# Attention weights of the first step and feed-forward weights of the last: transfers taken in turn, at most two or three large ones in flight

## The chip, the cores and the metric

One core of one Trainium2 chip. The metric is the device time of one execution in microseconds (us); lower is better. The granted clock, that is the share of TensorE's full clock that the throttle lets through, was 0.98 to 1.00 on the mean.

## The reference

Two passes over the same weights: attention with a recurrent memory, then a SwiGLU feed-forward. The attention goes through 64 segments of 32 tokens one after the other, 8 memory tokens in front of each, 32 heads of 128, model width 576, all weights bf16. Cut to what matters:

```python
def _A_ref(x, mem0, Wq, Wk, Wv, Wo, seg_len):          # 64 segments, in order
    for s in range(n_seg):
        h = jnp.concatenate([mem, xs], axis=1)         # 8 + 32 tokens, 576 wide
        q = jnp.einsum('btd,dhe->bhte', h, Wq)         # Wq, Wk, Wv: 576 x 32 x 128
        k = ...; v = ...
        ...                                            # masked softmax, o = p v
        o = jnp.einsum('bhte,hed->btd', o, Wo)         # Wo: 32 x 128 x 576
        mem = o[:, :M, :]
def _B_ref(x, w1, w3, w2):                             # 576 -> 4608 -> 576
    return jnp.einsum('bsf,fd->bsd', silu(x w1) * (x w3), w2)
x = x + _A_ref(_layernorm(x), ...)
x = x + _B_ref(_layernorm(x), ...)
x = x + _A_ref(_layernorm(x), ...)
x = x + _B_ref(_layernorm(x), ...)
```

## The kernel before

The kernel keeps all attention weights on the core and works in steps: one segment of each attention layer, the second layer seven steps behind the first, with feed-forward units between them to fill TensorE. The order of all instructions is planned ahead; small methods record them, so nearly every TensorE instruction has one source line (L538 before, L540 after the change) and every transfer of SyncE another. A transfer goes out in program order on SyncE's queue. There are two stretches that the change touches. At the **start**, SyncE issues all attention weights: 19 MB, without which the first step cannot go on. At the **end**, once Wv, Wq/Wk and Wo have been read for the last time, their places are loaded with the feed-forward weights of the last step, nine units of 1.77 MB:

```python
    def dma(self, out, in_):
        self.ch("SP", self.nc.sync.dma_start(out=out, in_=in_))
...
    def load_qk(self, kind):                       # Wq (0), then Wk (1)
        def f(n):
            wd = (self.a.wq, self.a.wk)[kind]
            for c in range(4):                     # four chunks of 128 rows, 1 MiB each
                self.dma(self.T.W[:, 4 * kind + c, :], wd[c * P:(c + 1) * P, :])
            self.dma(self.T.W[kind * R64:(kind + 1) * R64, 8, :], wd[4 * P:D, :])   # tail of 64 rows
        return f
...
    def load_o(self, g):                           # four of 1.18 MB
        return lambda n: self.dma(self.T.WO[:, g * GH:(g + 1) * GH, :],
                                  self.a.wo[g * GH:(g + 1) * GH].rearrange("h e d -> e h d"))
...
    def tail_load(self, i, what):                  # unit i of 9, last step
        def f(n):
            ...                                    # t13, t2: places in WV, W or WO
            if what != 1:
                for kind, wd in ((0, self.a.w1), (1, self.a.w3)):      # two of 512 KB
                    self.dma(t13[:, 4 * kind:4 * kind + 4], wd[0:4 * P, fa:fa + 512].rearrange("(c p) f -> p c f", p=P))
                for kind, wd in ((0, self.a.w1), (1, self.a.w3)):      # two small tails
                    self.dma(t13[kind * R64:(kind + 1) * R64, 8], wd[4 * P:D, fa:fa + 512])
            if what != 0:                                              # one of 576 KB
                self.dma(t2, self.a.w2[fa:fa + 512, :].rearrange("(b p) d -> p b d", p=P))
            ...
```

## Time and profile before

| | before |
|---|---|
| median of 3 runs | 2802.13 us (2796.95 to 2804.0) |
| profiled span | 2798.6 us |
| TensorE (PE) busy | 2730.5 us, 98% of the span |
| first matmul on the fourth Wk chunk | 26.86 us |
| first value matmul of step 1 (a mark behind the whole start) | 66.96 us |
| DMA share and rate, 4 to 30 us | 1.01, 377 GB/s |
| DMA share and rate, 2746 to 2786 us | 1.10, 337 GB/s |

The lines that bound the kernel are in the prediction.

The timeline of PE (start, us busy, what, count, in brackets the idle time before and what ended it) shows the last Wk chunk:

```profile
26.86 2.22 PE L538 MATMUL bank<-HT,W 128*128 128x40 bf16 x58 [2.50 <-DMA W<-in_A_Wk_dram]
```

### The profile page before, as it was taken

How to read it: one execution, taken by the hardware profiler on the slowest of the kernel's cores; microseconds unless marked ns; L12 is line 12 of the kernel's file. 1: busy time of each engine (PE TensorE's matmuls, PEld its weight loads, DVE VectorE, ACT ScalarE, POOL GpSimd, SP SyncE). 2: the span in 40 equal slices, each digit the busy share in tenths (PEclk: the TensorE clock that was granted, in tenths of full speed). 3: DMA queues.
4: the chain of work that ended last, by engine and by line, in shares of the span. 5: the costliest groups of instructions: out<-in, count | busy, mean ns of one | idle time of the engine just before them, and what ended most of it. 6: DMA issues, size and time to landing. Idle time of an engine off the chain costs nothing.

```text
span 2798.6 us, 136339 instructions
## 1 busy us (share of the span) xinstructions
PE 2730.5 (98%) x60909; PEld 2252.9 (81%) x60909; DVE 2018.1 (72%) x5501; ACT 1116.7 (40%) x3422; POOL 328.4 (12%) x399
## 2 busy tenths in 40 slices
PE   5999999999999999999999999999999999999998
PEld 4787878888888888888888888888888788888886
DVE  4677777777777677777767777776777777677765
ACT  2434443443434344343434434343443434343332
POOL 1111110110101011010101101010110101010110
PEclk9999999999999999999999999999999999999999
DMA  8072524234251523425152342515234251423568
GB/s 306 17 197 83 162 67 138 65 112 130 62 153 48 152 73 111 132 60 153 49 148 77 111 131 60 150 52 145 81 111 131 60 147 54 142 82 109 143 177 248
DMA packets 483438, 323.80 MB, mean 116 GB/s; under 512 B 26297, under 2 KB 478401, under 8 KB 481185
## 3 DMA queue, kind: packets, MB, share of 16 engines
q1 hardware_dynamic: 479824, 308.15, 37.6%
q8 instruction: 476, 7.80, 1.2%
q0 software_dynamic: 3024, 6.93, 0.8%
q14 instruction: 114, 0.93, 0.1%
HBM read 310.26 MB, written 2.36 MB: 112 GB/s over the span
## 4 chain that ended last, share of the span: by engine, by line
PE 96%; DMA 1%; ACT 1%; issue 1%; DVE 1%; POOL 0%; SPq 0%; DVEq 0%; ACTq 0%; POOLq 0%
PE bank L538 83%; PE YB L538 14%; DMA W<-in_A_Wk_dram 1%; ACT HT L541 0%; DMA W<-in_A_Wq_dram 0%; ACT OT L541 0%; DVE STAT L544 0%; DVE SME L544 0%; DVE PB L544 0%; ACT PTS L541 0%; DVE HTT L544 0%; ACT SME L541 0%; DVE PTS L544 0%; DVE XR L544 0%; DVE XN L544 0%
## 5 line engine op out<-in xcount | busy, mean ns | idle before, releaser
L538 PEld LDWEIGHTS <-W 128*128 128x128 bf16 (+1 forms) x29040 | 1227.2, 98 | 158.8 <-issue 53.6
L538 PE MATMUL bank<-HT,W 128*128 128x80 bf16 (+3 forms) x22720 | 815.5, 198 | 20.4 <-DMA W<-in_A_Wk_dram 11.7
L538 PE MATMUL bank<-XTB,W 128*128 128x256 bf16 (+3 forms) x6320 | 654.6, 262 | 1.4 <-issue 1.3
L895 POOL MEMSET PB<- 128x1024 bf16 x284 | 270.0, 951 | 2119.2 <-PE bank L538 1682.6
L541 ACT ACTIVATE QKT<-bank 128x64 bf16<-128x64 f32 (+1 forms) x1381 | 316.1, 315 | 364.2 <-PE bank L538 335.5
L538 PE MATMUL YB<-OT,WO 128*128 128x80 bf16 (+3 forms) x11360 | 429.4, 199 | 20.6 <-ACT HT L541 13.5
L538 PEld LDWEIGHTS <-WO 128*128 128x128 bf16 (+1 forms) x11400 | 389.0, 101 | 55.8 <-issue 39.3
L538 PE MATMUL bank<-WV,HT 128*32 128x512 bf16 (+1 forms) x6840 | 384.4, 382 | 0.0
L544 DVE CAST QKT<-bank 128x64 bf16<-128x64 f32 (+2 forms) x683 | 186.2, 316 | 238.7 <-PE bank L538 236.7
L541 ACT ACTIVATE HTT<-bank 128x512 bf16<-128x512 f32 (+1 forms) x324 | 177.8, 551 | 392.9 <-PE bank L538 391.5
L538 PE MATMUL bank<-W2C,HTT 128*128 128x288 bf16 x2232 | 320.7, 287 | 0.4 <-DMA W2C<-in_B_w_dram 0.4
L544 DVE TENSOR_REDUCE STAT<-SME 104x8 f32<-104x320 f32 (+1 forms) x568 | 271.8, 479 | 51.3 <-ACT SME L541 47.0
L544 DVE TENSOR_TENSOR PB<-SME,STAT 40x128 bf16<-40x128 f32 (+1 forms) x1004 | 283.5, 321 | 15.5
L538 PEld LDWEIGHTS <-HT 128*32 128x32 bf16 (+1 forms) x6840 | 149.4, 95 | 166.8 <-issue 42.8
L538 PEld LDWEIGHTS <-HTT 128*128 128x128 bf16 x2304 | 206.4, 98 | 59.2 <-issue 6.9
L544 DVE SCALAR_TENSOR_TENSOR XR<-bank,XR 128x288 f32<-128x288 f32 x576 | 239.6, 448 | 11.7 <-PE bank L538 7.2
L544 DVE SCALAR_TENSOR_TENSOR HTT<-HTT,bank 128x512 bf16<-128x512 bf16 (+1 forms) x324 | 201.9, 623 | 55.4 <-ACT HTT L541 53.4
L541 ACT ACTIVATE PTS<-bank 128x320 bf16<-128x320 f32 (+1 forms) x413 | 157.1, 414 | 177.6 <-PE bank L538 120.9
L544 DVE TENSOR_TENSOR HTT<-HTT,bank 128x512 bf16<-128x512 bf16 (+1 forms) x324 | 203.5, 628 | 22.3 <-PE bank L538 0.5
L541 ACT ACTIVATE OT<-bank 128x320 bf16<-128x320 f32 (+1 forms) x379 | 147.0, 412 | 171.1 <-PE bank L538 170.9
L541 ACT ACTIVATE SME<-SME 104x320 f32<-104x320 f32 (+1 forms) x284 | 133.5, 470 | 202.5 <-DVE SME L544 202.3
L544 DVE TENSOR_TENSOR SME<-bank,maskb 104x320 f32<-104x320 f32 (+1 forms) x284 | 133.9, 485 | 104.6 <-PE bank L538 102.8
(64 smaller groups left out, 1671.4 us busy)
## 6 DMA issues: line engine op xcount, KB each, us to landing
W<-in_B_w_dram SPq DMA_DIRECT2D x612, 256.0 KB, 3.8
W2C<-in_B_w_dram SPq DMA_DIRECT2D x306, 288.0 KB, 3.2
W<-in_B_w_dram SPq DMA_DIRECT2D x612, 32.0 KB, 3.4
W<-in_B_w_dram SPq DMA_DIRECT2D x10, 512.0 KB, 8.7
WO<-in_A_Wo_dram SPq DMA_DIRECT2D x4, 1152.0 KB, 18.3
XR<-in_A_x_dram POOLq DMA_DIRECT2D x16, 288.0 KB, 4.6
W<-in_A_Wq_dram SPq DMA_DIRECT2D x4, 1024.0 KB, 8.0
W<-in_A_Wk_dram SPq DMA_DIRECT2D x4, 1024.0 KB, 16.8
```

What stands on the lines that cost most here:

```text
L538: self.ch("PE", self.nc.tensor.matmul(out, lhsT=lhsT, rhs=rhs, start=start, stop=stop, skip_group_check=True, **k))
L541: self.ch("ACT", self.nc.scalar.activation(*a, **k))
L544: self.ch("DVE", getattr(self.nc.vector, fn_)(*a, **k))
L895: return lambda n: self.ch("POOL", self.nc.gpsimd.memset(self.T.PB[:, pb.i], 0.0))
```

## The change

The intent: let the large loads of both ends go out in turn. A large transfer waits until the one two before it (at the start) or three before it (at the end) has landed, so that SyncE's queue never holds more than two or three of them and other traffic, the instruction blocks above all, has less ahead of it. Below such a wait is called a gate: of two at the start, of three at the end. A transfer has landed, or is home, when all its bytes have arrived. No instruction of a compute engine is added or moved.

```diff
@@ in the constructor
         self.tail_w = {}
+        self.turn = []
+        self.turn_dep = mybir.DependencyInfo(mybir.DependencyClass.Sync, mybir.DependencyReason.DATA)
@@
     def dma(self, out, in_):
-        self.ch("SP", self.nc.sync.dma_start(out=out, in_=in_))
+        return self.ch("SP", self.nc.sync.dma_start(out=out, in_=in_))
+
+    def dma_in_turn(self, out, in_, depth):
+
+        inst = self.dma(out, in_)
+        if len(self.turn) >= depth:
+            self.tc.add_manual_dep(inst.ins, self.turn[-depth].ins.name, self.turn_dep, reason="transfers in turn")
+        self.turn.append(inst)
@@ load_qk (load_v and load_o likewise, each with depth 2)
-                self.dma(self.T.W[:, 4 * kind + c, :], wd[c * P:(c + 1) * P, :])
+                self.dma_in_turn(self.T.W[:, 4 * kind + c, :], wd[c * P:(c + 1) * P, :], 2)
@@ tail_load (likewise t2, the 576 KB)
-                    self.dma(t13[:, 4 * kind:4 * kind + 4], wd[0:4 * P, fa:fa + 512].rearrange("(c p) f -> p c f", p=P))
+                    self.dma_in_turn(t13[:, 4 * kind:4 * kind + 4], wd[0:4 * P, fa:fa + 512].rearrange("(c p) f -> p c f", p=P), 3)
```

The tails of 64 rows keep plain `dma` and are not counted.

More of the change, by code (lines that the diff above doesn't have):

```diff
@@ L604, in f @@
             for c in range(4):
-                self.dma(self.wv(False)[:, c, :], self.a.wv[c * P:(c + 1) * P, :])
+                self.dma_in_turn(self.wv(False)[:, c, :], self.a.wv[c * P:(c + 1) * P, :], 2)
             t = self.a.wv[4 * P:D, :].rearrange("p (k r n) -> p k r n", k=2, r=2)
@@ L611, in load_o @@
     def load_o(self, g):
-        return lambda n: self.dma(self.T.WO[:, g * GH:(g + 1) * GH, :],
-                                  self.a.wo[g * GH:(g + 1) * GH].rearrange("h e d -> e h d"))
+        return lambda n: self.dma_in_turn(self.T.WO[:, g * GH:(g + 1) * GH, :],
+                                          self.a.wo[g * GH:(g + 1) * GH].rearrange("h e d -> e h d"), 2)
     def load_xn(self, g, xn):
@@ L658, in f @@
             if what != 0:
-                self.dma(t2, self.a.w2[fa:fa + 512, :].rearrange("(b p) d -> p b d", p=P))
+                self.dma_in_turn(t2, self.a.w2[fa:fa + 512, :].rearrange("(b p) d -> p b d", p=P), 3)
             for h in range(2):
```

## The prediction

> **What bounds the kernel now.** I read the page first, then the waits of TensorE over the whole span and in its two ends, then the DMA issues of those ends, one by one, and last the timeline and the granted clock there. The page's busy line and the chain that ended last say that TensorE (PE) is the bound:
>
> ```profile
> PE 2730.5 (98%) x60909; PEld 2252.9 (81%) x60909; DVE 2018.1 (72%) x5501; ACT 1116.7 (40%) x3422; POOL 328.4 (12%) x399
> ...
> PE 96%; DMA 1%; ACT 1%; issue 1%; DVE 1%; POOL 0%; SPq 0%; DVEq 0%; ACTq 0%; POOLq 0%
> PE bank L538 83%; PE YB L538 14%; DMA W<-in_A_Wk_dram 1%; ACT HT L541 0%; DMA W<-in_A_Wq_dram 0%; ACT OT L541 0%; DVE STAT L544 0%; DVE SME L544 0%; DVE PB L544 0%; ACT PTS L541 0%; DVE HTT L544 0%; ACT SME L541 0%; DVE PTS L544 0%; DVE XR L544 0%; DVE XN L544 0%
> ```
>
> The reader should see that no DMA wait reaches 2% of the chain. The change touches only loads of the first 60 us and the last 60 us, some 4% of the span between them; the 2680 us in the middle keep their instructions, waits and buffers. So what there is to win or lose must be in PE's waits in those two stretches. PE's waits, first of the whole span (cut), then of 0 to 62 us, then of 2738 us to the end:
>
> ```profile
> PE bank L538 <- DMA W<-in_A_Wk_dram: 11.7, 5, 4.4
> PE bank L538 <- issue: 7.6, 8, 2.7
> PE YB L538 <- issue: 3.0, 2, 1.9
> ...
> PE bank L538 <- DMA W<-in_A_Wk_dram: 11.7, 5, 4.4
> PE bank L538 <- DVE XN L544: 10.2, 1, 10.2
> PE bank L538 <- issue: 5.4, 3, 2.7
> ...
> PE bank L538 <- DVE XN L544: 3.4, 1, 3.4
> PE YB L538 <- issue: 1.9, 1, 1.9
> PE bank L538 <- issue: 1.1, 1, 1.1
> ```
>
> Columns: total us, times, longest. Two things stand out. PE waits 11.7 us for the key weights at the start. And of its 7.6 + 3.0 = 10.6 us of "issue" gaps (nothing that the profile shows held it back) 5.4 + 1.9 + 1.1 = 8.4 us lie in the 120 us in which the DMA engines are full. I take these gaps to be late instruction blocks; the page's queue list has that traffic: 476 packets, 7.80 MB, that is 16.4 KB each. This is presumably what the change is after.
>
> How the start is loaded, from the DMA issues (size of each, median us from issue to landing; windows of half a microsecond, so mostly one transfer):
>
> ```profile
> XN<-in_A_x_dram SPq DMA_DIRECT2D x1, 144.0 KB, 2.1
> ...
> W<-in_A_Wq_dram SPq DMA_DIRECT2D x1, 1024.0 KB, 4.8
> ...
> W<-in_A_Wq_dram SPq DMA_DIRECT2D x1, 1024.0 KB, 11.6
> ...
> W<-in_A_Wk_dram SPq DMA_DIRECT2D x1, 1024.0 KB, 14.9
> ...
> W<-in_A_Wk_dram SPq DMA_DIRECT2D x1, 512.0 KB, 20.4
> ```
>
> The latency grows with the place in the queue, so the queue is served in order: Wq chunks issued at 1.62 to 3.1 us land at about 6.4, 9.0, 11.5 and 14.7, Wk chunks at 19.2, 21.7, 24.2 and 26.8 (PE's matmuls on them start at exactly such times), the 64-row tail at 29.4. The spacing of 2.5 us for 1.05 MB is 420 GB/s, and the DMA share of these stretches is 1.02: full. SyncE does not have an endless queue even now: it waits 10.3 us for landings of Wk and 9.5 us of Wq before it issues Wv and Wo, so about 8 transfers are out at a time.
>
> **What the Trainium skill says.** (1) "DMA: Bandwidth & Descriptors", section "Queues, rings and completion order": each engine goes round-robin between queue rows at packet granularity. Then an instruction block waits for a packet or so of the weights, not for the whole weights' queue, and a shorter queue would help it little so long as it is never empty. The trace does not contradict it: a load has 8 to 20 us of queue ahead of it at the start, the stalls are at most 2.7 us. (2) Same page, "Anatomy of one DMA": a transfer has a fixed part of about 2 us beside its bytes, and a semaphore wait is served by the issuing sequencer before dispatch. The trace agrees: 144 KB at 420 GB/s moves in 0.35 us and landed after 2.1 us, so 1.75 us are fixed. (3) "Runtime: NRT & Kernel Launch", "Instruction fetch mechanics": instructions stream in 16 KiB blocks through a DMA queue of their own; the 16.4 KB packets agree. (4) "TensorE: Matmul & The Clock Gate", Part 1: the clock halves after idleness. The trace agrees: the granted clock is 0.50 from 40 to 45 us and 0.53 from 2760 to 2765.
>
> **The change part by part.** It removes nothing and adds no instruction that runs on PE, DVE or ACT. It adds waits on SyncE alone.
>
> Start: 12 chunks of 1.05 MB (Wq, Wk, Wv) and 4 of 1.18 MB (Wo), each waits until the one two before it has landed; tails go ungated behind them. Costs: does the queue run dry? Chunk j is issued when j-2 has landed; then j-1 is still moving. A lone chunk needs about 4.8 us (the first Wq row above). In flow, two chunks take 2 x 2.5 = 5.0 us. So with a wake-up and issue of 0.1 to 0.4 us the loop is 4.9 to 5.2 us against 5.0: between 0 and 0.2 us lost for a pair. Before PE's Wk wait ends there are 8 chunks, and the two tails (2.5 us each) refill the margin where they fall; I count +1 us, range 0 to 3, on the path. Gain: 4.5 of the 5.4 us of gaps sit at 33.9 (1.8) and 39.8 (2.7), after Wk has landed. Even if they vanished, PE would run into the next loads: Wv's fourth chunk lands at about 42.2 (issued 19.2, 23.0 to land) and PE starts on Wv at 44.0; Wo's last lands at 57.0 (issued 44.3, 12.7 to land) and PE reads it at about 58. So at most 1 to 2 us of those 4.5 can be had while the stream keeps its rate; with the round-robin rule I expect half of it, -1 us.
>
> End: 9 units of 1.77 MB, in each three large transfers (512, 512, 576 KB) gated three back, two small ones free. About one unit is in flight at a time; when its first part lands, 512 + 576 KB and more are still to move, 3.4 us at 330 GB/s, against 1.75 us fixed. The queue never runs dry: cost 0. What it could win is the 1.9 + 1.1 us of gaps. But the end is tied to the stream as well:
>
> ```profile
> 2778.88 0.52 SPq L547 DMA_DIRECT2D WO<-in_B_w_dram  x1
> WO<-in_B_w_dram SPq DMA_DIRECT2D x1, 512.0 KB, 8.6
> ...
> 2789.46 2.68 PE L538 MATMUL bank<-XTB,WO 128*128 128x128 bf16 x40
> ```
>
> The last unit's first part lands at 2787.5, its second (issued 2779.4, 9.7 to land) at about 2789.2; PE reaches the unit at 2789.46 and needs the second part four matmuls later. Slack: 0.4 us. Removing 3 us of gaps at 2746 to 2754 would only make PE wait here. -0.3 us.
>
> Sum: +1 - 1 - 0.3 = -0.3 us on a mean of the three runs of (2802.13 + 2796.95 + 2804.0) / 3 = 2801.0. **Predicted: 2801 us.**
>
> **Rivals.** (a) *The instruction fetch is freed and the loads speed up*: if long queues delay the fetches, and if 16 engines kept in step bring each chunk home earlier (by 29.4 us 10.1 MB had moved by the slices' rates, where 9.6 MB were needed, so half a megabyte of later loads, 1.1 us, ran ahead), then up to 4.5 + 3.0 + 1.1 = 8.6 us go: 2792. For it: the gaps lie almost wholly under full queues. Against it: Wv, Wo and the last unit have 0.4 to 2 us of slack. (b) *The gate becomes a new wait*: if landing to first byte takes 1 us more than I think, a chunk loses about 0.5 us, and the 8 to 16 gated chunks of the start cost 4 to 8 us, since every load there follows the last closely: 2805 to 2809. For it: 4.8 against 5.0 us is hardly any margin. Against it: the tails in between, and three in flight while they pass. (c) *All of it is hidden*: 2801.
>
> **Range and chances.** The three runs of before span 7 us alone. (a) and (b) are of like size and opposite sign, so 2793 to 2809 should hold it 8 times in 10. A 2% change is 56 us. The two ends together are 120 us and PE is busy for more than half of it, and all DMA waits and gaps there sum to some 22 us, so no reading reaches 56: faster 0.01, within 2% 0.98, slower 0.01.
>
> **What would show it.** Right: landings from issue of about 5 us for the start's chunks (not 8 to 21), but PE's matmuls on the last Wk chunk and tail within 2 us of 26.9 and 29.4; the wait of PE for Wk near 12 us; SyncE's waits for DMA grown; issue gaps in the first 62 us still 3 us or more; PE at the last unit between 2788 and 2791 relative to this trace. Wrong towards (a): gaps under 2 us in both ends, and the DMA's rate there above 420 and 330 GB/s. Wrong towards (b): the DMA share under 0.9 between 5 and 30 us, and Wk's tail after 32 us.

## More of the kernel before

The page's list of DMA issues gives for each group of transfers the size of each and the median us from issue to landing:

```profile
WO<-in_A_Wo_dram SPq DMA_DIRECT2D x4, 1152.0 KB, 18.3
...
W<-in_A_Wq_dram SPq DMA_DIRECT2D x4, 1024.0 KB, 8.0
W<-in_A_Wk_dram SPq DMA_DIRECT2D x4, 1024.0 KB, 16.8
```

A megabyte that is 17 us on its way at 420 GB/s has waited in a queue: it is the length of the queue that these figures show.

## The result, and the profile after

| | before | after |
|---|---|---|
| median of 4 runs each, same rounds | 2801.5 us (2796.95 to 2804.0) | 2806.02 us (2805.15 to 2807.35) |
| ratio after / before | | 1.0018, 95% interval 1.0001 to 1.0036 |
| profiled span | 2798.6 us | 2805.6 us |
| PE: fourth Wk chunk | 26.86 us | 30.99 us |
| PE: first score matmul | 30.89 us | 34.90 us |
| PE: first value matmul of step 1 | 66.96 us | 70.40 us |
| DMA share, 4 to 30 us | 1.01 | 0.93 |
| DMA share, 2746 to 2786 us | 1.10 | 1.01 |

Here and below a ratio is the mean time of one kernel's runs over the mean of the other's in the same rounds, so not quite the ratio of the medians. The change is "the same" within 2%, but about 5 us slower. All outputs are right.

The chain that ended last, after:

```profile
PE 94%; DMA 4%; ACT 1%; DVE 1%; issue 0%; SPq 0%; POOL 0%; DVEq 0%; ACTq 0%
```

Before, PE had 96% and DMA 1%. The 3% more are some 80 us: the chain now follows the loads through both ends, where it followed PE. That tells which way the bound runs there; it is not the size of the loss. PE's waits between 0 and 70 us, after (us in total, times, longest):

```profile
PE bank L540 <- DMA W<-in_A_Wk_dram: 12.3, 4, 4.5
...
PE bank L540 <- DMA W<-in_A_Wq_dram: 4.7, 2, 3.4
PE bank L540 <- issue: 4.2, 2, 2.9
```

The wait for Wk has hardly grown (11.7 before), but the wait for Wq has, from 1.7 to 4.7 us: the loss begins at the very first chunks. The gaps "issue" are still there. SyncE's own waits in the same stretch, after:

```profile
SPq L549 <- DMA W<-in_A_Wq_dram: 13.7, 4, 4.3
SPq L549 <- DMA WV<-in_A_Wv_dram: 11.7, 4, 4.3
SPq L549 <- DMA W<-in_A_Wk_dram: 11.2, 4, 4.3
SPq L549 <- DMA WO<-in_A_Wo_dram: 9.5, 3, 5.3
```

So the gates do what they should: SyncE now waits some 46 us for landings in place of 20, and the page's transfers are 7 to 8 us on their way in place of 8 to 18:

```profile
WO<-in_A_Wo_dram SPq DMA_DIRECT2D x4, 1152.0 KB, 8.3
W<-in_A_Wq_dram SPq DMA_DIRECT2D x4, 1024.0 KB, 7.3
W<-in_A_Wk_dram SPq DMA_DIRECT2D x4, 1024.0 KB, 7.1
```

7.1 and 7.3 us can be read as 2 x 2.5 us for two chunks in flight and 2.1 to 2.3 us of fixed time (an estimate from the spacing of 2.5 us). What that buys is in the timeline of PE, after, to set beside the line of before at 26.86:

```profile
17.79 0.21 PE L540 MATMUL bank<-HT,W 128*128 128x40 bf16 x1 [3.44 <-DMA W<-in_A_Wq_dram]
...
30.99 3.98 PE L540 MATMUL bank<-HT,W 128*128 128x40 bf16 x105 [3.31 <-DMA W<-in_A_Wk_dram]
```

The last Wk chunk comes 4.1 us later. The engines were not full all the time, as two of the stretches of 1 us show (length, busy us and count of PE, PEld, DVE, ACT, POOL, then granted clock, DMA share, GB/s). Before:

```profile
22.00:23.00 1.00, 0.00 (x0) 0.00 (x0) 0.00 (x0) 0.00 (x0) 0.00 (x0) 1.00 0.98 410
```

After:

```profile
22.00:23.00 1.00, 0.22 (x1) 0.11 (x1) 0.00 (x0) 0.00 (x0) 0.00 (x0) 1.00 0.08 33
23.00:24.00 1.00, 0.00 (x0) 0.00 (x0) 0.00 (x0) 0.00 (x0) 0.00 (x0) 1.00 0.49 123
```

A share of 0.08 is hardly more than one engine of 16 (0.06). The trace's records of single packets say the same: from 22.4 to 23.3 us only one packet at a time is in progress, 8 KB packets of 309 ns one after the other: one engine alone still moves its part of a chunk, and 15 engines have nothing, for the next chunk may not be issued before that last part is home. Packets take 309 ns in both kernels; no engine has become slower.

At the end, the last unit of the last step. The timeline of PE after (its counterpart before, 40 matmuls in one piece from 2789.46, is in the prediction):

```profile
2793.36 0.60 PE L540 MATMUL bank<-XTB,WO 128*128 128x128 bf16 x4 [2.31 <-DMA WO<-in_B_w_dram]
...
2794.84 3.93 PE L540 MATMUL bank<-XTB,WO 128*128 128x128 bf16 x36 [0.88 <-DMA WO<-in_B_w_dram]
```

and a stretch of the same execution:

```profile
2795.00:2800.00 5.00, 5.00 (x42) 3.75 (x41) 1.52 (x4) 0.77 (x2) 0.00 (x0) 0.50 0.02 7
```

PE waits 3.2 us for the weights of the last unit where it waited for none, and runs at a granted clock of 0.50 afterwards: 36 matmuls take 3.93 us where 40 took 2.68 before, and the next 8 on W 1.80 us in place of 1.15.

The 7.0 us between the two profiled executions, step by step: +3.4 at the start; -1.3 in the middle, where the execution of before has one gap of 1.1 us that the other lacks (chance: the instructions there are the same); -0.8 because PE's gaps at 2747 and 2754 are 1.4 + 0.8 us in place of 1.1 + 1.9; +0.3 up to the last unit; +3.2 of waiting there; +2.2 of halved clock. These sum to 7.0.

### The profile page after: what moved, and what is told of

Its sections match the earlier page's. It is cut to its first block, busy times and chain, and to the rows that moved or that the text cites. A ratio compares the mean times of both kernels' runs of the same rounds, so it can differ in the third digit from the quotient of the medians.

```text
span 2805.6 us, 136351 instructions
## 1 busy us (share of the span) xinstructions
PE 2733.6 (97%) x60909; PEld 2254.8 (80%) x60909; DVE 2018.9 (72%) x5501; ACT 1117.4 (40%) x3422; POOL 328.8 (12%) x399
## 4 chain that ended last, share of the span: by engine, by line
PE 94%; DMA 4%; ACT 1%; DVE 1%; issue 0%; SPq 0%; POOL 0%; DVEq 0%; ACTq 0%
PE bank L540 81%; PE YB L540 13%; DMA W<-in_B_w_dram 1%; DMA WO<-in_A_Wo_dram 1%; DMA W<-in_A_Wq_dram 1%; DMA WV<-in_A_Wv_dram 1%; DMA W<-in_A_Wk_dram 0%; ACT HT L543 0%; DMA WO<-in_B_w_dram 0%; ACT OT L543 0%; DMA WV<-in_B_w_dram 0%; DVE STAT L546 0%; DVE PB L546 0%; DVE SME L546 0%; DVE XR L546 0%
## 5 line engine op out<-in xcount | busy, mean ns | idle before, releaser
L540 PE MATMUL bank<-HT,W 128*128 128x80 bf16 (+3 forms) x22720 | 815.2, 198 | 22.3 <-DMA W<-in_A_Wk_dram 12.3
```

The costliest lines, as they stand in the source:

```text
L540: self.ch("PE", self.nc.tensor.matmul(out, lhsT=lhsT, rhs=rhs, start=start, stop=stop, skip_group_check=True, **k))
```

## The experiments

**The theory** after reading the two traces: a gate waits for the whole chunk, and a chunk is home when the slowest of its 16 engines is. "DMA: Bandwidth & Descriptors" of the Trainium skill, section "Why a DMA increments its semaphore by 16 and not by 1", says that each engine's last descriptor adds 1 to the semaphore after its own data; the trace agrees, with 16 packets of four bytes at the end of each transfer. As long as the queue is long, an engine that lags costs the others nothing, since they go on with the next chunk. With a gate of two there is a margin of only about 0.1 us (estimate: when a chunk lands the next has 2.5 us left to move, and the loop from landing over issue to the first bytes takes 4.9 - 2.5 = 2.4 us, by the lone chunks of g2 below), and every lag beyond it is idleness of all the other engines. It foretells that a gate one deeper, with a margin of 2.6 us, costs nothing.

**Rivals.** One: it is the start of the transfers that takes longer than reckoned (the loop, not the lag); then depth 1 must be slower than its own 4.8 us for each chunk. Two: only one of the two ends does harm. Three, on the gain that did not come: the gaps of PE have nothing to do with the DMA queues, or they have, and the gate of two or three leaves the engines just as full.

To weigh them I worked out, from each trace's records of single packets, how long an engine was idle on the mean of the 16, once in the start's stretch and once in the end's. (The records do not name the engine: idle is how far the number of packets in progress lies below 16. Counted more finely, the figures move by up to 0.1 us.)

| kernel (depth at start / end; - is no gate) | idle us, 4 to 56 us | idle us, 2746 to 2786 us | PE: fourth Wk chunk, us |
|---|---|---|---|
| before (- / -) | 0.00 | 0.00 | 26.86 |
| e3_deeper (4 / 6) | 0.00 | 0.01 | 27.64 |
| g4_one_more (3 / 4) | 0.02 | 0.24 | 28.65 |
| e2_tail_only (- / 3) | 0.01 | 2.51 | 29.82 |
| h2_tail_again (- / 3) | 0.00 | 2.33 | 27.30 |
| after (2 / 3) | 2.56 | 1.59 | 30.99 |
| g1_after_again (2 / 3) | 2.34 | 2.05 | 32.70 |
| e1_start_only (2 / -) | 4.17 | 0.08 | 31.30 |
| h1_start_again (2 / -) | 3.07 | 0.25 | 30.60 |
| g2_one_at_a_time (1 / 1) | 15.24 | (window holds other loads) | 40.88 |

And the times. "Difference" is the mean of the kernel's runs less the mean of the runs of before:

| kernel | median us (runs) | before, same rounds | difference us | ratio, 95% |
|---|---|---|---|---|
| e1_start_only | 2803.83 (5) | 2800.79 | +3.1 | 1.0011, 0.9999 to 1.0024 |
| h1_start_again | 2804.39 (5) | 2802.62 | +2.3 | 1.0009, 0.9995 to 1.0022 |
| e2_tail_only | 2800.87 (5) | 2800.79 | +1.4 | 1.0005, 0.9993 to 1.0018 |
| h2_tail_again | 2802.67 (5) | 2802.62 | +1.3 | 1.0005, 0.9993 to 1.0018 |
| g1_after_again | 2806.81 (5) | 2802.11 | +5.1 | 1.0019, 1.0007 to 1.0032 |
| g4_one_more | 2801.36 (5) | 2802.11 | -1.1 | 0.9997, 0.9985 to 1.001 |
| e3_deeper | 2799.49 (5) | 2800.79 | -1.8 | 0.9995, 0.9982 to 1.0009 |
| g2_one_at_a_time | 2884.49 (2) | 2802.11 | +82.3 | 1.0295, 1.0276 to 1.0313 |
| g3_tails_together | 2804.82 (5) | 2802.11 | +2.3 | 1.0009, 0.9995 to 1.0022 |
| e4_v_late | 2811.35 (2) | 2800.79 | +10.4 | 1.0038, 1.0019 to 1.0056 |

### Each end alone

e1_start_only is the change with its end undone, e2_tail_only with its start undone. h1_start_again and h2_tail_again are the same two kernels, run again on another chip.

```diff
 e1, h1: in tail_load (both places)
-  ..., 3)
+  ..., 99)
 e2, h2: in load_qk, load_v, load_o
-  ..., 2)
+  ..., 99)
```

> The gate of two on the attention weights of the first step alone; the last step's loads go as before. Theory A (each gated issue waits for the slowest of the 16 DMA engines, so the others run dry; both gates cost): the trace shows step 1's first value matmul at about 70.4 us as in the changed kernel (67.0 before), moments with under 4 of the 16 engines at work around 22 to 23 us, and no wait of TensorE for the last unit's weights at the end; time +2 to +4 us over the kernel before. Rival B (only the gate at the end costs, the later start is made good in the middle): time within 1 us of before although the start is late. Rival C (a short queue brings instruction blocks sooner): issue gaps of TensorE in the first 70 us well under the 5.9 us of before, under 3; if the gaps are again over 4 us, C falls.

> The gate of three on the feed-forward weights of the last step alone; the start as before. Theory A: step 1's first value matmul at 67.0 us as before; at the end the load stream runs some 5% slower (about 318 GB/s against 335), TensorE waits 2 to 4 us for the last unit's weights, and what follows that wait runs at half the granted clock; time +3 to +6 us over before. Rival B' (the wait at the end is only a consequence of what the late start shifted, or chance of one execution): no wait for the last unit over 1 us, time within 1 us of before. Rival C: the two issue gaps before the last step's end (1.1 and 1.9 us before) shrink to under 1 us in sum.

> The gate of two at the start alone, once more, to part the two gates' shares. If the start carries most of the loss (first run: 2803.83 against 2800.79 us): again +2 to +4.5 us; again the completions of the third chunk by the 16 engines spread over about 2 us or more where the kernel before has 0.5; TensorE's first matmul on Wk's last chunk after 29 us (26.9 before).

> The gate of three at the end alone, once more. First run: two of five executions 3 to 5 us slower, three equal to before. If the gate only costs when the engines' lag passes the slack of the last unit: again a mixed picture, mean +0.5 to +3 us, idle engine time between 2746 and 2786 us of 1.5 us or more (of all 16) where the ungated end has under 0.1; if the first run's two slow executions were chance, all five lie within 1 us of before.

Measured: the start alone +3.1 and +2.3 us, the end alone +1.4 and +1.3 us; e2's is well under its expected +3 to +6. Each interval holds 1, so no single one of the four is proof; but the pairs agree, and 2.7 + 1.3 = 4.0 us is near the 5.1 us of both. In the traces the parts are clear. With the start's gate alone PE's fourth Wk chunk comes at 31.30 and 30.60, and the engines are idle 4.2 and 3.1 us there, but the last unit finds its weights at hand:

```profile
2794.45 2.68 PE L540 MATMUL bank<-XTB,WO 128*128 128x128 bf16 x40
```

With the end's gate alone (e2) it does not:

```profile
2791.40 0.40 PE L540 MATMUL bank<-XTB,WO 128*128 128x128 bf16 x4 [1.99 <-DMA WO<-in_B_w_dram]
...
2793.05 3.93 PE L540 MATMUL bank<-XTB,WO 128*128 128x128 bf16 x36 [1.25 <-DMA WO<-in_B_w_dram]
```

The end's loss is not the same in each execution. The five runs of e2 are 2805.69, 2803.63, 2800.87, 2800.65 and 2800.52; the profile is of the first, so the lines above show the end at its worst. In h2, whose profiled run was its fastest (2801.19), PE still waits 2.28 us in that place, but no half clock follows. Only one execution of each kernel has a trace, so what the end does in the other fast ones is left open. Rival two falls by the traces: each gate alone makes PE wait for late weights at its own end. By the times the start costs about twice as much, but the end's +1.3 us is not clear of zero by itself.

### The same again

g1_after_again is the change itself, unaltered, on another chip.

> The changed kernel once more, for a second trace and a closer interval. Theory A (waiting for the slowest of 16 DMA engines leaves the others dry, at a moment that differs between executions): again +3 to +6 us over before; again moments in the first 30 us with few of the 16 engines at work, though not at the same microsecond as in the first trace; a wait for the last unit's weights at the end in some executions. If the first trace's hole at 22 to 23 us was chance, no second with under 8 engines at work shows between 5 and 30 us, and the loss is not in the start.

Measured: +5.1 us, interval clear of 1, so the loss is real. Its trace has 2.34 us of idle engines at the start and a fourth Wk chunk at 32.70. At its end PE does not wait for weights at the last unit, but it does one unit earlier, for 2.03 us, and the granted clock falls to 0.66 in the 5 us from 2790: the 36 matmuls behind the wait take 3.33 us, where 36 of the same kind took 2.07 in e2 at full clock.

```profile
2790.55 3.33 PE L540 MATMUL bank<-XTB,W 128*128 128x128 bf16 x36 [2.03 <-DMA W<-in_B_w_dram]
```

So all four traces with the gate of three (after, g1, e2, h2) have PE waiting 2.0 to 3.2 us for the weights of one of the last two units, three of them with a lowered clock behind it; without that gate or with a deeper one the wait is 0.4 us (g4) or none.

### One deeper, and deeper still

```diff
 g4_one_more: load_qk, load_v, load_o; tail_load
-  ..., 2)      -  ..., 3)
+  ..., 3)      +  ..., 4)
 e3_deeper
-  ..., 2)      -  ..., 3)
+  ..., 4)      +  ..., 6)
```

> The change with one more transfer in flight at either end: 3 at the start, 4 at the end. Theory A: a third chunk of 1 MiB gives a late engine 2.5 us of room, so most of the loss goes: time +0 to +2 us over before, no moment with under 8 engines at work between 5 and 30 us. Rival: any gate costs the same 4 us.

> The same change with 4 in flight at the start and 6 at the end. Theory A: with two more chunks queued on each engine a late engine holds nobody up: all 16 engines at work from 4 to 30 us, Wk's last chunk lands within 0.5 us of before (26.9), the stream at the end at 330 GB/s or more, no wait for the last unit over 0.5 us; time within 1.5 us of before. Rival D (the added semaphore waits on SyncE themselves cost, whatever the depth): still +2 us or more.

Measured: -1.1 and -1.8 us, neither to be told from zero (both a little under what was expected, 0 to +2 and within 1.5; e3's fourth Wk chunk is 0.8 us behind that of before, where 0.5 was expected). The rival that any gate costs, by its semaphore waits alone, falls with them. One step deeper takes the idleness at the start from 2.3 to 4.2 us down to 0.02, and at the end from 1.6 to 2.5 down to 0.24. That is the sharp step the theory wants: no gradual gain, but a margin that is either larger than the lag of the engines or not. The sizes fit as well. The four traces with a gate of two have 3.0 us of idle engines at the start on the mean and their fourth Wk chunk at 31.4; the five with none or a deeper one have none and, with e4 below (29.11, no idleness up to there), 28.2. That is 3.2 us later for 3.0 us of idleness, against 2.7 us of time by e1 and h1. The last unit of e3 is whole again:

```profile
2786.77 2.68 PE L540 MATMUL bank<-XTB,WO 128*128 128x128 bf16 x40
```

### One at a time

```diff
 g2_one_at_a_time: all gated loads
-  ..., 2)      -  ..., 3)
+  ..., 1)      +  ..., 1)
```

> The suspected cost doubled: one large transfer in flight at either end. If a gated chunk costs a whole loop of landing, issue and first byte (4.8 us for 1 MiB at the start, some 3.2 us for 512 KB at the end by the traces) in place of its share of the stream (2.5 and 1.6 us), the first step's output weights land at about 83 us (57 before), step 1's first value matmul comes at about 93 us (67.0 before), and the end grows by some 36 us; together about 2862 us, between 2845 and 2880. If the engines' queues hid that loop, the time stays within 10 us of the changed kernel.

This measures the loop by itself: chunk out, home, next issue. The page's DMA issues:

```profile
W<-in_A_Wq_dram SPq DMA_DIRECT2D x4, 1024.0 KB, 4.9
...
W<-in_B_w_dram SPq DMA_DIRECT2D x10, 512.0 KB, 4.0
```

4.9 us for a lone megabyte is what the prediction took (4.8), so rival one falls at the start: the loop was right there. Step 1's first value matmul comes at 95.08 us, 28 us late, as expected. At the end a lone 512 KB takes 4.0 us and not the 3.2 I had expected; the end lost some 54 us more, and the total of 2884.49 lies above the expected range. Depth 1 at the end is therefore dearer than I thought, and it puts the margin of three in flight at about 0.9 us (estimate: two parts, 1.05 to 1.11 MB, are 3.2 to 3.4 us at 330 GB/s, against 4.0 less 1.6 us of its own bytes, 2.4). By the landing records of the end's transfers, 2746 to 2790 us, the first and the last engine lie 1.7 to 2.0 us apart in the median with the gate of three (2.5 us before), so the lag eats that, too.

How large are the lags? The 16 completion packets of the third Wq chunk, the first one that the gate holds back, landed at these times:

| kernel | first to last, us |
|---|---|
| before | 10.6 to 11.0 |
| e3_deeper (4) | 10.7 to 11.2 |
| g4_one_more (3) | 10.7 to 11.4 |
| h2_tail_again (-) | 10.7 to 11.2 |
| e2_tail_only (-) | 10.5 to 12.0 |
| after (2) | 10.7 to 13.4 |
| g1_after_again (2) | 11.0 to 12.9 |
| e1_start_only (2) | 11.1 to 13.3 |
| h1_start_again (2) | 10.8 to 13.0 |

In the trace of after, 15 of the 16 are home by 11.24; the last engine finished its part of the second chunk at 8.98 and began its part of the third at 11.16, although that had been issued at 6.6. So with a gate of two the lag is 1.9 to 2.7 us at this place in all four traces (one engine is late in after and e1, two in g1 and h1), against 0.5 to 0.7 in all but one of the others listed. A long queue does not keep the engines together either: from the loads of Wv on, and at the end, they lie about 2 us and more apart in before as well, and there it costs nothing, since no engine runs dry. **Why** one or two engines start the first gated chunk 2 us late is not shown by any record, and stays open. The one exception, e2, is instructive: an engine lagged there with no gate, PE had its Wk chunk late (29.82), but the other engines went on with later loads and were idle for 0.01 us.

### The gaps of PE: the values' weights held back

e4_v_late takes the kernel before and holds the loads of Wv and Wo back until PE has done the query and key matmuls of step 0, so that the DMA engines are empty while PE runs through them. It asks whether the "issue" gaps come from full queues at all.

```diff
 load_v, load_o
-    self.dma(...)
+    self.hold((out, in_))          # recorded, not issued
 qk_tail, last key unit of step 0
+    if t == 0 and u == 7:
+        self.let_go()              # issue them; the first waits for PE's last matmul so far
```

> From the kernel before: the value and output weights of the first step are held back until TensorE has done all query and key matmuls of step 0, so that the DMA engines are almost empty from 30 to about 43 us. It is slower on purpose (12 us or more, the loads come later). It asks what makes TensorE's issue gaps at 33.9 and 39.8 us (1.8 and 2.7 us before, 1.2 and 2.9 with the change). If full DMA queues delay the instruction blocks, the gaps of this stretch vanish: under 1 us in sum. If TensorE runs through a block of instructions faster than the next can come even on idle engines, they stay: 3 us or more in sum.

Before, 30 to 35 us, columns as above:

```profile
30.00:35.00 5.00, 3.94 (x132) 3.59 (x129) 3.33 (x11) 1.44 (x6) 0.00 (x0) 1.00 1.01 416
```

e4:

```profile
30.00:35.00 5.00, 5.00 (x149) 4.66 (x146) 2.15 (x6) 0.96 (x4) 0.00 (x0) 1.00 0.01 3
```

With the engines empty (share 0.01) PE is busy without a break. Its waits in the first 70 us of e4:

```profile
PE bank L539 <- DMA WV<-in_A_Wv_dram: 9.2, 5, 4.0
...
PE bank L539 <- issue: 0.2, 1, 0.2
```

The gaps, 5.9 us before, are gone but for 0.2 us; PE then waits 9.2 us for the values' weights, and the whole is 10.4 us slower (12 or more was expected). The clean part of the test is the two large gaps of before, 4.5 us together: where they would fall, at 36.0 and 39.6 us of e4, PE runs through without a wait. So the first half of rival three falls: the gaps do come from full DMA engines. What the gates do to them shows when the gaps of all traces are set side by side (PE's waits for "issue"; start 0 to 70 us, end from 2738 us):

| gates | start's gaps, us | end's gaps, us |
|---|---|---|
| none in that stretch | 5.9 (before), 5.8 (e2), 3.9 (h2), 6.0 (g3) | 3.0 (before), 3.0 (g3), 3.3 (e1), 3.5 (h1), 3.4 (e4) |
| deep | 4.4 (e3), 4.7 (g4) | 2.9 (e3), 2.3 (g4) |
| 2 at the start, 3 at the end | 4.2 (after), 3.7 (g1), 2.3 (e1), 1.6 (h1) | 2.2 (after), 1.9 (g1), 1.1 (e2), 2.4 (h2) |
| 1 | 0.7 (g2) | none (g2) |

The gate of two takes some 2.4 us of 5.4 (3.0 on the mean), that of three some 1.3 of 3.2 (1.9 on the mean). The intent was not empty, then: e1's sign for it, start gaps under 3 us, came true. But on the whole the gaps go as the engines run dry: a gate that keeps the engines full (e3, g4) keeps most of the gaps, and one that empties them takes away more in late weights than it gives in early instructions.

In the trace of before the two gaps at 33.9 and 39.8 us go with two packets of 16,384 bytes on the instruction queue, begun at 33.24 and 39.67 and lasting 1.02 and 1.33 us; PE resumes 1.45 us after each has ended. The packets of e4 show where the time goes. PE enters the block before the late one at 29.96 us in before and at 31.68 in e4; the late block's packet begins 3.3 us after that in before, but 0.4 us in e4 (for the second gap 4.0 and 0.3 us). The packet itself is hardly shorter on idle engines, 0.88 to 1.06 us. So the time is lost before the packet begins, some ten times the 309 ns of one packet of weights, and with a queue that is shorter but never empty (e3, g4) it is still 2.9 to 5.1 us. That fits an engine that serves its queues by turns, as the prediction's first citation has it: a shorter line ahead helps little, an engine with nothing else to do helps fully. What exactly the packet waits for is argued, not shown.

### Both tails at once

g3_tails_together takes the kernel before and sends the 64-row tail of Wq (partitions 0 to 63) from ScalarE's queue, as soon as Wk's third chunk is home, so that it goes beside Wk's tail (partitions 64 to 127). It asks whether the order of the loads at the start, rather than the length of the queue, has something to give.

```diff
 load_qk(0)
-    self.dma(self.T.W[0:R64, 8, :], wq[4 * P:D, :])
 qk, t == 0 and u == 0
+    nc.scalar.dma_start(out=W[0:R64, 8, :], in_=wq[4 * P:D, :])   # waits for Wk's third chunk
```

> From the kernel before, without gates: the 64-row tail of Wq goes out on ScalarE's queue together with Wk's tail on SyncE's. In the trace each tail moves at 205 to 240 GB/s (8 KB packets of 610 ns in place of 309), as if half of the way into SBUF were used. If the two tails, in the two halves of the partitions, can move at once, Wk's part lands 1.5 to 2.5 us earlier (PE passes 29.4 at about 27.5) and the time falls by 0 to 2 us. If the engines visit the two halves in step, the packets stay at 610 ns and nothing is won.

Measured: +2.3 us, not to be told from zero; the hoped gain did not come. PE's timeline in g3:

```profile
24.89 2.08 PE L538 MATMUL bank<-HT,W 128*128 128x40 bf16 x57 [2.86 <-DMA W<-in_A_Wk_dram]
33.10 1.63 PE L538 MATMUL bank<-HT,W 64*128 64x40 bf16 x48 [6.13 <-DMA W<-in_A_Wq_dram]
```

The Wk chunks come 2 us earlier, as they should with half a megabyte less ahead of them, but the tail comes only at 33.10 (29.41 before). From 24 to 32 us, 2 us at a time, g3 moves 213, 328, 238 and 229 GB/s at a share of 1.0. Before, a stretch in which one tail of 64 rows went alone (26 to 28 us) had 225 GB/s, and a chunk of 128 rows some 420: a tail fills the engines at about half the rate, and with both tails under way the rate was no better. "DMA: Bandwidth & Descriptors", section "Rules for kernel authors", says of two transfers to disjoint partition halves "Don't bother — they serialize"; this run agrees.

No version beats the kernel before: e3 and g4 are level with it.

## Why the prediction was right or wrong

**The result within 2%, and the range.** Right: 2806.02 lies in 2793 to 2809, and the bound on the whole (PE at 98%, only the two ends touched) held. That the range held the result was partly luck: it was widened to 2809 for a loop that is 1 us longer, and the loss came from something else.

**The sum, -0.3 us.** Wrong in sign: about +5. Term by term:

- *Start's gate, +1 us (0 to 3).* Mis-sized: +2.7 us by e1 and h1, gaps that shrank included, with the fourth Wk chunk 3.2 us late on the mean. The working, 4.9 to 5.2 us of loop against 5.0, had the right loop (4.9 by g2). **The step that failed is "between 0 and 0.2 us lost for a pair"**: it set the mean stream beside a lone chunk's loop as though a chunk were one thing. It is 16 parts, the gate waits for the last, and the parts lay 1.9 to 2.7 us apart at the first gated chunk. The prediction had even said that there was "hardly any margin" (rival b), and gave it too little weight.
- *End's gate, "The queue never runs dry: cost 0".* Wrong: 1.6 to 2.5 us of idle engines with the gate of three, 0.3 or less without, +1.3 us of time (from nothing to about 5). The 1.75 us of fixed time was that of a small transfer (it rests on the trace alone: the section cited beside it gives its 2 us for transfers that GpSimd issues, and these are SyncE's); with a 512 KB one alone it is 4.0 less 1.6, so 2.4, and the margin shrinks from the 1.7 I had (3.4 less 1.75) to 0.9.
- *Start's gaps, -1 us.* About right in kind: 4.2 us in place of 5.9 in this pair, some 2.4 us less on the mean of the traces. How much of it reached the end cannot be told apart from the gate's cost. The reason given (a shorter queue helps little while it is never empty) holds by e3 and g4, and e4 shows its other half; but a block waited 2.9 and 3.6 us longer under full queues, not "a packet or so" of 0.3 us.
- *End's gaps, -0.3 us.* They shrank by 0.8 us in this pair, and PE then waited for the last unit, as foreseen in kind; but it waited 3.2 us and not the rest of a small slack.

**The rivals.** The time is rival (b)'s, 2805 to 2809. Its mechanism is not: it wanted a landing-to-first-byte longer by 1 us, and g2 shows that the loop is not longer at the start; only the one or two late engines began that late. The gate did become a new wait, by way of the lag. Rival (a) is out: no load came earlier, the rates fell (337 to 319 GB/s at the end). Its premise, that full queues hold the fetches up, is confirmed by e4. Rival (c) is out by the 5 us.

**The signs.** Chunks "about 5 us from issue" measured 7.1 to 8.3: I gave the time of a lone chunk where two are in flight. Wk within 2 us of 26.9 and its tail within 2 us of 29.4: 30.99 and 33.35, failed, and this was the sign that told the truth. PE's wait for Wk near 12: 12.3, right, and useless, since the loss sat in the wait for Wq. SyncE's waits grown, and gaps of 3 us or more: right. PE at the last unit between 2788 and 2791: 2793.36 with its wait. The sign "towards (b)", a DMA share under 0.9 between 5 and 30 us, did not fire at 0.92 although the harm was done: 4 us of trouble in 25 is spread too thin in a mean. Its second half, Wk's tail after 32 us, did fire: PE's first matmul on that tail comes at 33.35 us, 0.13 us after the one before it, where it came at 29.41.

## What to carry to other kernels

A limit on transfers in flight must be set by the slowest of the DMA engines and not by the mean rate: when a transfer lands, those still in flight must cover the whole loop of landing, issue and first bytes *and* the lag between engines, here 2.4 us and about 2 us or more of lag. Take one more than the arithmetic asks for (three megabytes in flight cost nothing here where two cost 3 us), and do not expect a limit that keeps the engines full to help the instruction fetch much. To see such idleness, look at stretches of 1 us or count idle time engine by engine; a mean over the stage hides it.

## What the Trainium skill lacked or had wrong

- "DMA: Bandwidth & Descriptors" lacks how many transfers must be in flight to keep the engines full. Here, with 1 MiB each, an engine was idle 15.2 us of 52 with one in flight, 2.3 to 4.2 us with two, 0.02 with three and 0.00 with four.
- The same page says that the engines finish independently, but not by how much they lie apart: at the third chunk 0.5 to 0.7 us in a long queue as a rule and 1.9 to 2.7 us behind a gate of two, in all four traces; late in a long queue, at the end of before, 2.5 us in the median. The cause of that lag is on no page and in no run here.
- "Runtime: NRT & Kernel Launch" calls the crossing of an instruction block "mostly hidden". Under full DMA queues two crossings cost PE 1.8 + 2.7 us here, and with empty engines nothing (e4); the block's packet began 3.3 and 4.0 us after PE had entered the block before it, against 0.3 to 0.4 us. It also gives PE room for 2048 instructions; the two gaps lie only 128 matmuls and their weight loads, 256 instructions, apart, so that here no such store bridged a late block.
- "DMA: Bandwidth & Descriptors" was right that two transfers to disjoint partition halves gain nothing, but has no figure for the pair: here both together ran at 229 to 238 GB/s (28 to 32 us of g3), where one alone had 225 and whole chunks 420.
